# Attention times input weights as seven block products for batches 2 to 4, their right operands split once and kept in scratch memory

## The chip, the cores and the metric

The kernel runs on one core of a Trainium2 chip. The metric is the device time of one execution in microseconds (us), lower is better. The engines named below are PE (TensorE: matmuls; PEld are its weight loads), DVE (VectorE), ACT (ScalarE), POOL (GpSimd) and SP (SyncE); POOL and SP only issue DMAs in the part that is changed.

## The reference

Four batches (b = 0 to 3) of q, k and v with N = 6080 rows and C = 256 columns; the attention is over channels, so its matrix is 256 x 256. The result of the attention goes through a feed-forward layer with squared ReLU.

```python
qn = q / (norm(q, axis=1) + 1e-6)          # per batch and column
kn = k / (norm(k, axis=1) + 1e-6)
a  = softmax(kn.T @ qn / tau)              # 256 x 256 per batch; the sum has + 1e-9
x  = v @ a                                 # 6080 x 256
h  = x @ w_in                              # w_in 256 x 2048
out = (maximum(h, 0) ** 2) @ w_out         # w_out 2048 x 256
```

## The kernel before

The kernel doesn't compute x. For each batch it folds the attention into the weights, W = a @ w_in (256 x 2048), and takes h = v @ W. Every matmul operand that must be exact is split into a high and a low fp32r part, and a product is three matmuls, high by high, high by low and low by high.

The rows of a batch are cut into six chunks, five of T = 512 and one of T = 480 column pairs (1024 or 960 rows, 24 chunks in all), and the 2048 columns of W into eight blocks j. A chunk with a block is a **quad**, the unit in which all is placed: 192 quads, numbered 0 to 191, 48 to a batch. Layer 1 of a quad is a Strassen-Winograd product of 2 x 2 blocks: seven block products m1 to m7 of three matmuls each (`product`, L395), whose results pass PSUM banks named h, x and z and are summed by ACT copies (x L429, z L438, m L450) and DVE adds (s L455). ACT and DVE square the ReLU and split it into g high and g low (r L404/L405, g L406/L407 and, for the second half, L416 on DVE, g high L417 on ACT, g low L418 on DVE). Layer 2 (`layer2`, L490) takes 24 matmuls of a quad's g with wo's high and low half (woh, wol), one quad later, on the output banks o. That is 45 matmuls to a quad.

The block sums that layer 1 needs of W are made by `combine` for a **group** g of two blocks: DVE adds, then for each of the two blocks a weight tile wt that ACT casts (L323, high halves) and DVE subtracts (L324, low halves), stored by POOL to the scratch wsc (L326). Each quad loads its weight tile from there on SP's queue (`load_wt`, L332), issued 1.5 quads ahead. wt is a ring of three buffers that these tiles under construction share with the loaded ones.

While a batch runs, the next batch b is prepared beside it. `at(u, f, ...)` hands f to the scheduler at u, in quads; with end = 30 + 48 (b - 1), the scores (L180, 12 matmuls of 256 columns a quad) run up to quad `end`, then norms, exps and `attnT` (transposes, quad end + 2.46). Then comes the fold of the four groups: their inputs are loaded (`load_win`, SP), split into high and low (`fold_split`, ring hl, L286/L287) and multiplied in two halves of six matmuls each (`fold`, L302), one half in each of two quads; the result is scaled by the softmax's denominator as ACT copies it from PSUM (L305, buffer kqt). MID is 0.46.

The order of the instructions on each engine is fixed at build time by the scheduler from these places. The rings that matter are wt (3 buffers), kqt (3), hl (3), sq (2), and two PSUM banks h. SP and POOL issue their DMAs in program order, and a DMA that has to wait holds up those behind it.

Of the kernel before, what the change touches and what calls it, by code (L numbers as in the profile page):

```python
# [8 lines left out]
F32 = mybir.dt.float32  # L9
F32R = mybir.dt.float32r  # L10
# [6 lines left out]
P = 128  # L17
# [3 lines left out]
def tile_channel_attention_relu2_ffn(ctx, tc, kq, vT, tau, w_in, w_out, outT):  # L21
# [85 lines left out]
    win = {}  # L107
# [33 lines left out]
    kqt = {}  # L141
# [41 lines left out]
    def score_add(b, s):  # L183
        if b in s_acc:
            nc.vector.tensor_add(out=s_acc[b], in0=s_acc[b], in1=s)
        else:
            s_acc[b] = small.tile([P, NH * C], F32, name="s_acc")
            nc.vector.tensor_copy(out=s_acc[b], in_=s)

    def score_burst(b, kts):  # L190
# [13 lines left out]
    def norms(b):  # L204
        a = accs[b][:, 0]
        nc.vector.tensor_add(out=a, in0=a, in1=accs[b][:, 1])
        nps = h_bank()
        for i in range(2 * NH):
            nc.tensor.matmul(out=nps[:, i:i + 1], lhsT=a[:, i * P:(i + 1) * P], rhs=ones[:, 0:1],
                             start=True, stop=True)  # L210
        n2 = nps[:, :2 * NH]
        y = small.tile([P, 2 * NH], F32, name="y")
        z = small.tile([P, 2 * NH], F32, name="z")
        nc.scalar.activation(out=y, in_=n2, func=AF.Sqrt)
        nc.scalar.activation(out=root, in_=y[:, 0:1], func=AF.Exp, scale=0.0)
        x = y
        y = small.tile([P, 2 * NH], F32, name="y2")
        nc.vector.tensor_scalar_max(out=y, in0=x, scalar1=1e-30)
        nc.vector.reciprocal(out=z, in_=y)
        nc.vector.tensor_mul(out=z, in0=z, in1=n2)  # L220
        nc.vector.tensor_add(out=y, in0=y, in1=z)
        nc.vector.tensor_scalar(out=y, in0=y, scalar1=0.5, scalar2=1e-6, op0=ALU.mult, op1=ALU.add)
        nc.vector.reciprocal(out=z, in_=y)
        nc.vector.tensor_scalar_mul(out=z[:, :NH], in0=z[:, :NH], scalar1=rtau)
        diag = small.tile([P, NH, P], F32, name="diag")
        for d in range(NH):
            nc.vector.tensor_scalar_mul(out=diag[:, d], in0=ident, scalar1=z[:, NH + d:NH + d + 1])
        attn[b, "z"] = z, diag
# [10 lines left out]
    def exps(b, s):  # L239
        z, zq = attn[b, "z"]  # L240
        den = small.tile([P, NH], F32, name="den", bufs=2)
        attn[b, "e"] = []
        for h in range(NH):
            e = small.tile([P, C], F32, name="e", bufs=2)
            nc.vector.scalar_tensor_tensor(out=e, in0=s[:, h * C:(h + 1) * C], scalar=z[:, h:h + 1],
                                           op0=ALU.mult, in1=zq, op1=ALU.mult)
            nm = small.tile([P, 1], F32, name="nm", bufs=2)
            nc.vector.tensor_reduce(out=nm, in_=e, op=ALU.max, axis=AX.X, negate=True)
            nc.scalar.activation(out=e, in_=e, func=AF.Exp, bias=nm, scale=1.0, accum_out=den[:, h:h + 1])
            attn[b, "e"].append(e)  # L250
        nc.vector.tensor_scalar_add(out=den, in0=den, scalar1=1e-9)
        nc.vector.reciprocal(out=den, in_=den)
        attn[b, "den"] = den

    def attnT(b):
        aT = h_bank()
        aTv = aT.rearrange("p (d c) -> p d c", d=NH)
        for h, e in enumerate(attn[b, "e"]):
            for d in range(NH):
                nc.tensor.transpose(out=aTv[:, d, h * P:(h + 1) * P], in_=e[:, d * P:(d + 1) * P],  # L260
                                    identity=ident)
        aTh = small.tile([P, NH, C], F32R, name="aTh")
        aTl = small.tile([P, NH, C], F32R, name="aTl")
        nc.scalar.copy(out=aTh, in_=aTv)
        nc.vector.tensor_sub(out=aTl, in0=aTv, in1=aTh)
        attn[b] = aTh, aTl


    NP = 7
    A11, A12, A22, S2, S3, S1, S4 = range(NP)  # L270
    wt = {}
    wi = {}
    us = {}
    wsc = {}

    def load_win(b, g):
        win[b, g] = work.tile([P, NH, 2, GW], F32, name="kqt", tag="kqt", bufs=KB)
        nc.sync.dma_start(out=win[b, g], in_=wins[g])

    def fold_split(b, g):  # L280
        W = win.pop((b, g))
        wi[b, g] = []
        for d in range(NH):
            w = work.tile([P, 2, 2 * GW], F32R, name="hl", tag="hl", bufs=HB)
            x = W[:, d].rearrange("p t f -> p (t f)")
            (nc.vector.tensor_copy if b else nc.scalar.copy)(out=w[:, 0], in_=x)  # L286
            nc.vector.tensor_sub(out=w[:, 1], in0=x, in1=w[:, 0])  # L287
            wi[b, g].append(w)

    def fold(b, g, ch, ps=None):  # L290
        aTh, aTl = attn[b]
        if ch == 0:
            tag, n = ("kqt", KB) if b or g else ("vt", VB)
            us[b, g] = work.tile([P, NH, 2, GW], F32, name=tag, tag=tag, bufs=n)
        u = us[b, g]
        cs = slice(ch * P, (ch + 1) * P)
        if ps is None:
            ps = h_bank()
        n = 0
        for d in range(NH):  # L300
            for l, r in ((aTh, 0), (aTh, 1), (aTl, 0)):
                nc.tensor.matmul(out=ps, lhsT=l[:, d, cs], rhs=wi[b, g][d][:, r, :],  # L302
                                 start=n == 0, stop=n == 3 * NH - 1)
                n += 1
        nc.scalar.activation(out=u[:, ch].rearrange("p t f -> p (t f)"), in_=ps, func=AF.Copy,  # L305
                             scale=attn[b, "den"][:, ch:ch + 1])

    def combine(b, g):

# [8 lines left out]
        for i in range(2):  # L318
            j = 2 * g + i
            w = work.tile([P, 2, NP, P], F32R, name="wt", bufs=WB)  # L320
            js = slice(i * P, (i + 1) * P)
            for o, x in ((w[:, :, 0:2], u[:, :, 0, js]), (w[:, :, 2:3], u[:, 1:2, 1, js]), (w[:, :, 3:7], S[:, :, js])):
                nc.scalar.copy(out=o[:, 0], in_=x)  # L323
                eng.tensor_sub(out=o[:, 1], in0=x, in1=o[:, 0])  # L324
            wsc[b, j] = scratch.tile([P, 2, NP, P], F32, name=f"wsc{j}", bufs=2)
            nc.gpsimd.dma_start(out=wsc[b, j], in_=w.bitcast(F32))  # L326
# [13 lines left out]
    vt = {}  # L340
# [190 lines left out]
    s1 = ps_o.tile([P, HMAX], F32, name="o11")  # L531
# [48 lines left out]
    for b in range(1, B):  # L580
        u0 = (b - 1) * QB
        first, last = (NJ + 2 if b == 1 else 0), 30
        for i in range(NT // 2):
            u, k = u0 + first + i * (last - first) // (NT // 2), 2 * i
            if k % G == 0:
                at(u - 3.4, score_load, b, k // G)
            at(u - 0.8, score_norm, b, k)
            if b > 1 or k >= EARLY * G:
                at(u - 1.0, score_split, b, k)
                at(u - 0.5, score_split, b, k + 1)  # L590
                at(u + MID, score_burst, b, [k, k + 1])
        end = u0 + last
        at(end + MID, norms, b)
        at(end + 1 + MID, spread, b)
        at(end + 1.6, lambda b=b: exps(b, s_acc[b]))
        at(end + 2 + MID, attnT, b)
        for g in range(NG):
            u = end + 3 + 4 * g
            at(u - 3.0, load_win, b, g)
            at(u - 0.5, fold_split, b, g)  # L600
            at(u + MID, fold, b, g, 0)
            at(u + 1 + MID, fold, b, g, 1)
            at(u + 1.7, combine, b, g)
    for n, (ci, j) in enumerate(quads):
        if ci:
            at(n - 1.5, load_wt, ci, j)
# [61 lines left out]
```

## Time and profile before

| | |
|---|---|
| median of 3 runs | 2172.79 us (2172.06 to 2174.04) |
| the profiled execution | 2172.03 us, its span 2170.2 us |
| granted TensorE clock | 1.00 |
| PE busy | 2156.8 us, 99% of the span |
| DVE, ACT, POOL busy | 1568.7, 1389.2 and 70.1 us |
| DMA | 323.08 MB, mean 149 GB/s |

The profiled execution is 0.76 us below the median, and its span starts and ends inside it: 1.8 us lie around the span. Matmuls overlap, so the length of one (0.39 us) is not what it costs; that is read from start to start.

### The profile page before, as it was taken

Reading aid. Unit: us, or ns where it says so; the run is one execution under the profiler, and the core shown is the slowest. Engines: PE = TensorE matmul, PEld = TensorE weight load, DVE = VectorE, ACT = ScalarE, POOL = GpSimd, SP = SyncE. Lnnn points to the kernel's source line nnn. Section 1 sums busy time; section 2 is a strip of 40 time slices with the busy share of each in tenths; the row PEclk is TensorE's granted clock in tenths of the full one; section 3 lists DMA queues with packets and bytes.
Section 4 is the critical chain, followed back from the end, with each engine's and each line's share of the span. In section 5 each row is a group of like instructions: output and inputs, shape, how many; then the busy total and the mean of one; then the engine's idle time right before and its main releaser. Section 6 shows DMA issues by size and latency. Waiting matters only on the chain.

```text
span 2170.2 us, 26050 instructions
## 1 busy us (share of the span) xinstructions
PE 2156.8 (99%) x9908; PEld 1806.2 (83%) x9908; DVE 1568.7 (72%) x2252; ACT 1389.2 (64%) x2359; POOL 70.1 (3%) x135
## 2 busy tenths in 40 slices
PE   9999999999999999999999999999999999999999
PEld 8778888888888888888888888888888888888887
DVE  6897788776787777876678778777677666666665
ACT  5786767666666666665676766666566565566564
POOL 0000000000000000000000000000000000000000
PEclk9999999999999999999999999999999999999999
DMA  9755534245364343334535434333344342343331
GB/s 341 269 199 182 192 114 153 84 167 193 125 217 151 134 162 106 115 113 148 187 144 209 163 124 148 112 124 133 129 154 156 133 141 105 104 140 104 104 122 53
DMA packets 61917, 323.08 MB, mean 149 GB/s; under 512 B 7328, under 2 KB 9888, under 8 KB 55008
## 3 DMA queue, kind: packets, MB, share of 16 engines
q1 hardware_dynamic: 49440, 266.03, 35.4%
q0 software_dynamic: 12352, 55.39, 6.5%
q8 instruction: 78, 1.28, 0.2%
q14 instruction: 47, 0.39, 0.1%
HBM read 265.03 MB, written 56.36 MB: 148 GB/s over the span
## 4 chain that ended last, share of the span: by engine, by line
PE 62%; issue 32%; DVE 2%; DMA 1%; POOL 1%; ACT 1%; SPq 0%; POOLq 0%; DVEq 0%; ACTq 0%
PE o L490 30%; PE h L395 15%; PE z L395 8%; PE x L395 4%; PE h L180 2%; PE x L180 2%; PE h L302 1%; POOL outT L496 1%; DMA kqt<-kq 1%; POOL wsc L326 0%; DMA wsc<-wt 0%; DVE vt L373 0%; DVE s L455 0%; DVE wt L324 0%; DVE hl L101 0%
## 5 line engine op out<-in xcount | busy, mean ns | idle before, releaser
L490 PE MATMUL o<-g,woh 128*128 128x512 f32 (+1 forms) x3072 | 1065.4, 388 | 1.9 <-DVE g L418 1.0
L490 PEld LDWEIGHTS o<-g,woh 128*128 128x128 f32 x3072 | 576.0, 188 | 120.6 <-DVE g L418 2.2
L395 PE MATMUL h<-vt,wt 128*128 128x512 f32 (+1 forms) x2304 | 614.9, 388 | 1.5 <-ACT x L429 1.5
L490 PE MATMUL o<-g,wol 128*128 128x512 f32 (+1 forms) x1536 | 594.8, 387 | 0.0
L395 PEld LDWEIGHTS h<-vt,wt 128*128 128x128 f32 x2304 | 431.7, 188 | 91.1 <-ACT x L429 3.4
L417 ACT CAST g<-s 128x1024 fp32r<-128x1024 f32 (+1 forms) x192 | 199.1, 1037 | 320.4 <-DVE s L416 320.1
L407 DVE TENSOR_TENSOR g<-r,g 128x512 fp32r<-128x512 f32 (+1 forms) x384 | 263.1, 685 | 155.6 <-ACT g L406 150.9
L490 PEld LDWEIGHTS o<-g,wol 128*128 128x128 f32 x1536 | 288.3, 188 | 57.2
L395 PE MATMUL z<-vt,wt 128*128 128x512 f32 (+1 forms) x1152 | 324.8, 389 | 0.4 <-ACT z L438 0.4
L418 DVE TENSOR_TENSOR g<-s,g 128x1024 fp32r<-128x1024 f32 (+1 forms) x192 | 233.0, 1213 | 123.1 <-ACT g L417 122.5
L405 ACT ACTIVATE r<-r 128x512 f32<-128x512 f32 (+1 forms) x384 | 241.2, 628 | 6.9
L395 PEld LDWEIGHTS z<-vt,wt 128*128 128x128 f32 x1152 | 212.1, 188 | 39.3 <-ACT z L438 0.8
L404 ACT ACTIVATE r<-z 128x512 f32<-128x512 f32 (+1 forms) x192 | 113.3, 590 | 202.3 <-PE z L395 201.0
L416 DVE SCALAR_TENSOR_TENSOR s<-s 128x1024 f32<-128x1024 f32 (+1 forms) x192 | 232.3, 1210 | 1.1
L406 DVE CAST g<-r 128x512 fp32r<-128x512 f32 (+1 forms) x192 | 81.8, 426 | 188.3 <-ACT r L405 187.4
L395 PE MATMUL x<-vt,wt 128*128 128x512 f32 (+1 forms) x576 | 160.8, 387 | 0.0
L455 DVE TENSOR_TENSOR s<-z,m 128x512 f32<-128x512 f32 (+1 forms) x192 | 130.5, 680 | 19.7 <-PE z L395 19.6
L438 ACT COPY z<-h 128x512 f32<-128x512 f32 (+1 forms) x192 | 110.3, 574 | 50.7 <-PE h L395 50.3
L161 DVE TENSOR_TENSOR acc<-acc,sq 128x1024 f32<-128x1024 f32 x92 | 112.7, 1225 | 28.8 <-ACT sq L160 26.5
L455 DVE TENSOR_TENSOR s<-h,m 128x512 f32<-128x512 f32 (+1 forms) x192 | 130.2, 678 | 0.0
L395 PEld LDWEIGHTS x<-vt,wt 128*128 128x128 f32 x576 | 108.1, 188 | 21.6
L404 ACT ACTIVATE r<-x 128x512 f32<-128x512 f32 (+1 forms) x192 | 113.6, 592 | 10.2
(112 smaller groups left out, 1757.3 us busy)
## 6 DMA issues: line engine op xcount, KB each, us to landing
wt<-wsc SPq DMA_DIRECT2D x184, 896.0 KB, 4.6
kqt<-kq SPq DMA_DIRECT2D x47, 1024.0 KB, 6.6
wsc<-wt POOLq DMA_DIRECT2D x32, 896.0 KB, 5.5
v<-vT SPq DMA_DIRECT2D x40, 512.0 KB, 5.6
outT<-res POOLq DMA_DIRECT2D x80, 256.0 KB, 5.0
g<-kq SPq DMA_DIRECT2D x6, 1024.0 KB, 10.5
kqt<-wins SPq DMA_DIRECT2D x12, 512.0 KB, 6.6
v<-vT SPq DMA_DIRECT2D x8, 480.0 KB, 4.4
```

What stands on the lines that cost most here:

```text
L161: nc.vector.tensor_add(out=accs[b], in0=accs[b], in1=sq)
L180: nc.tensor.matmul(out=s[:, h * C:(h + 1) * C], lhsT=l, rhs=r, start=first and h == 0 and n == 0, stop=last and n == len(terms) - 1, skip_ ...
L395: nc.tensor.matmul(out=out[:, :T], lhsT=w[:, l, i], rhs=v[:, r, :T], start=start and n == 0, stop=n == 2, skip_group_check=True)
L404: nc.scalar.activation(out=r[:, :T], in_=ps[:, :T], func=AF.Relu)
L405: nc.scalar.activation(out=r[:, :T], in_=r[:, :T], func=AF.Square)
L407: nc.vector.tensor_sub(out=hl[:, 1, :T], in0=r[:, :T], in1=hl[:, 0, :T])
L416: nc.vector.scalar_tensor_tensor(out=s, in0=s, scalar=0.0, op0=ALU.max, in1=s, op1=ALU.mult)
L417: nc.scalar.copy(out=h, in_=s)
L418: nc.vector.tensor_sub(out=l, in0=s, in1=h)
L438: nc.scalar.copy(out=st["Z"][:, :T], in_=st["B"][:, :T])
L455: ins = nc.vector.tensor_add(out=state[q]["s"][:, i, :T], in0=ps[:, :T], in1=state[q]["m7"][:, :T])
L490: nc.tensor.matmul(out=o[:, :T], lhsT=l[:, wg, wj, es], rhs=r[:, :T], start=first and k == 0, stop=last and k == 2)
```

## The change

Batch 0 is folded as before. For b = 1 to 3 the groups are taken in two **pairs** (g = 0 and 2, with u = end + 3 and end + 10), and each pair's 256 x 512 by blocks is one Strassen-Winograd product of 2 x 2 blocks: seven products of three matmuls, 512 columns wide (`fold7`, L362), one product in each of 14 quads in a row. The left operands, seven 128 x 128 blocks or block sums of the attention's transpose, are made and split in `attnT`. The right operands are blocks and block sums of w_in; `right7` makes and splits them for b = 1 and stores the split tiles to a scratch tsc on POOL's queue, and for b = 2 and 3 loads them from there on SP's queue, 2.5 quads ahead. DVE adds and ACT copies collect the seven results. The softmax's denominator is applied to e on DVE, ahead of the transposes. `combine` is unchanged, but both groups of a pair are now combined one after the other at the pair's end (quads end + 10 and end + 10.6; end + 17 and end + 17.6), where before each group was combined in its own second quad (end + 4.7, and every fourth quad on). The tiles diag and e move into another ring.

```diff
     def attnT(b):
...
+        a11, a12, a21, a22 = a[:, 0, :P], a[:, 1, :P], a[:, 0, P:], a[:, 1, P:]
+        nc.vector.tensor_add(out=s1, in0=a21, in1=a22)
+        nc.vector.tensor_sub(out=s2, in0=s1, in1=a11)
+        nc.vector.tensor_sub(out=s3, in0=a11, in1=a21)
+        nc.vector.tensor_sub(out=s4, in0=a12, in1=s2)
+        for o, x in ((w[:, :, 0:2], a[:, :, :P]), (w[:, :, 2:3], a[:, 1:2, P:]), (w[:, :, 3:7], S)):
+            nc.scalar.copy(out=o[:, 0], in_=x)
+            nc.vector.tensor_sub(out=o[:, 1], in0=x, in1=o[:, 0])
+        attn[b] = w
...
+    ORDER = (A11, A12, S4, S2, S1, S3, A22)
...
+    def right7(b, g, k):
+        hl = right[b, g, k] = work.tile([P, 2, 2 * GW], F32R, name="hl", tag="hl", bufs=HB)
+        if b > 1:
+            nc.sync.dma_start(out=hl.bitcast(F32), in_=tsc[g, k])
+            return
...
+        nc.scalar.copy(out=hl[:, 0], in_=x)
+        nc.vector.tensor_sub(out=hl[:, 1], in0=x, in1=hl[:, 0])
+        if B > 2:
+            tsc[g, k] = scratch.tile([P, 2, 2 * GW], F32, name=f"tsc{g}_{k}")
+            nc.gpsimd.dma_start(out=tsc[g, k], in_=hl.bitcast(F32))
+
+    def fold7(b, g, k):
+        i = ORDER[k]
+        r = right.pop((b, g, k))
+        ps = h_bank()
+        for n, (l, m) in enumerate(((0, 0), (0, 1), (1, 0))):
+            nc.tensor.matmul(out=ps, lhsT=attn[b][:, l, i], rhs=r[:, m], start=n == 0, stop=n == 2)
...
+        if i == A11:
+            nc.scalar.copy(out=U, in_=ps)
+        elif i == A12:
+            add(out=c11, in0=U, in1=ps)
+        elif i == S4:
+            nc.scalar.copy(out=c12, in_=ps)
+        elif i == S2:
+            add(out=U, in0=U, in1=ps)
+        elif i == S1:
+            add(out=V, in0=U, in1=ps)
+            add(out=c12, in0=c12, in1=V)
+        elif i == S3:
+            add(out=c22, in0=V, in1=ps)
+            add(out=U, in0=U, in1=ps)
+        else:
+            add(out=c21, in0=U, in1=ps)
...
-        for g in range(NG):
-            u = end + 3 + 4 * g
-            at(u - 3.0, load_win, b, g)
-            at(u - 0.5, fold_split, b, g)
-            at(u + MID, fold, b, g, 0)
-            at(u + 1 + MID, fold, b, g, 1)
-            at(u + 1.7, combine, b, g)
+        for g in range(0, NG, 2):
+            u = end + 3 + 3.5 * g
+            if b == 1:
+                at(u - 3.5, load_wins2, g)
+            for i in range(NP):
+                at(u + i - (0.7 if b == 1 else 2.5), right7, b, g, i)
+                at(u + i + MID, fold7, b, g, i)
+            at(u + NP, combine, b, g)
+            at(u + NP + 0.6, combine, b, g + 1)
```

Three places show how instructions move. Names carry the number of a tile; the lines of the changed kernel are L362 (fold7), L404 (casts of combine), L407 (stores), L413 (weight loads), L476 (layer 1), L571 (layer 2).

On PE, the middle of a quad with a fold before (the second half of a group of batch 1):

```order
L490 MATMUL o_3752<-g_4154,wol 128x512
L490 MATMUL o_3752<-g_4154,woh 128x512
L302 MATMUL h<-hl,aTh 128x512 x2
L302 MATMUL h<-hl,aTl 128x512
L302 MATMUL h<-hl,aTh 128x512 x2
L302 MATMUL h<-hl,aTl 128x512
L395 MATMUL z<-vt,wt 128x512 x3
L395 MATMUL h<-vt,wt 128x512 x3
```

and the same quad after:

```order
L571 MATMUL o_3763<-g_4167,wol 128x512
L571 MATMUL o_3763<-g_4167,woh 128x512
L362 MATMUL h<-hl,aT 128x512 x3
L476 MATMUL z<-vt,wt 128x512 x3
L476 MATMUL h<-vt,wt 128x512 x3
```

Six matmuls have become three, at the same place of the quad.

On PE, quad 49 before, from the product x to the score matmuls (L180) of batch 2; each o takes the matmuls with g's high part (woh), wol, and last the low part of g with woh:

```order
L395 MATMUL x<-vt,wt 128x512 x3
L490 MATMUL o_5251<-g_5205,woh 128x512
L490 MATMUL o_5251<-g_5205,wol 128x512
L490 MATMUL o_5251<-g_5205,woh 128x512
L490 MATMUL o_5255<-g_5205,woh 128x512
L490 MATMUL o_5255<-g_5205,wol 128x512
L490 MATMUL o_5255<-g_5205,woh 128x512
L180 MATMUL h<-hl 128x256 x12
L395 MATMUL z<-vt,wt 128x512 x3
```

and after:

```order
L476 MATMUL x<-vt,wt 128x512 x3
L180 MATMUL h<-hl 128x256 x4
L571 MATMUL o_5324<-g_5278,woh 128x512
L571 MATMUL o_5324<-g_5278,wol 128x512
L571 MATMUL o_5328<-g_5278,woh 128x512
L571 MATMUL o_5328<-g_5278,wol 128x512
L180 MATMUL h<-hl 128x256 x8
L476 MATMUL z<-vt,wt 128x512 x2
L571 MATMUL o_5324<-g_5278,woh 128x512
L571 MATMUL o_5328<-g_5278,woh 128x512
L476 MATMUL z<-vt,wt 128x512
```

The two matmuls with the low part of g have moved behind all score matmuls and two of z.

On ACT, the casts of a weight tile that waits for the store of the one before, and what stands behind them, before (the group at quads 34 and 35):

```order
L323 CAST wt_3906<-kqt_3776 128x256 [waits DMASW4_49,DVE_49]
L323 CAST wt_3906<-kqt_3776 128x128
L323 CAST wt_3906<-sq_3892 128x512
L404 ACTIVATE r_3995<-z_3951 128x512 [waits DVE_49,PE_49]
L417 CAST g2_3979<-s_3971 128x1024 [waits DVE_49]
L429 COPY x_4008<-h_4004 128x512 [waits PE_49]
```

and after (the second group of the first pair, quads 41 and 42):

```order
L404 CAST wt_4481<-kqt_3796 128x256 [waits DMASW3_49,DVE_49]
L404 CAST wt_4481<-kqt_3796 128x128
L404 CAST wt_4481<-sq_4476 128x512 [waits DVE_49]
L485 ACTIVATE r_4605<-z_4549 128x480 [waits DVE_49,PE_49]
L404 CAST wt_4490<-kqt_3796 128x256 [waits DMAHW3_49,DMAHW0_49]
L404 CAST wt_4490<-kqt_3796 128x128
L404 CAST wt_4490<-sq_4476 128x512
L510 COPY x_4618<-h_4614 128x480 [waits PE_49]
```

The cast that waits for a store (a DMASW semaphore) is now followed by another tile's casts ahead of the copy x. On SP, the weight loads of quads 41 to 44 are after:

```order
L413 DMA wt_4348<-wsc1_430 128x1792 [waits DMAHW0_49,PE_49]
L427 DMA v_4414<-vT 128x1024 [waits DVE_49]
L427 DMA v_4414<-vT 128x1024 [waits DMAHW5_49]
L413 DMA wt_4466<-wsc2_632 128x1792 [waits DMAHW1_49,DMASW6_49,DMAHW6_49,DVE_49,PE_49]
L148 DMA kqt_4853<-kq 128x2048 [waits DVE_49]
L413 DMA wt_4581<-wsc3_641 128x1792 [waits DMASW5_49,DMAHW2_49,DMASW3_49,PE_49]
L413 DMA wt_4669<-wsc4_855 128x1792 [waits DMASW6_49,DMAHW3_49,DVE_49,PE_49]
```

and before:

```order
L332 DMA wt_4346<-wsc1_431 128x1792 [waits DMAHW7_49,PE_49]
L346 DMA v_4389<-vT 128x1024 [waits DMAHW3_49,DVE_49,Activation_49]
L346 DMA v_4389<-vT 128x1024
L332 DMA wt_4435<-wsc2_633 128x1792 [waits DMASW7_49,DMAHW6_49,DMASW6_49,Activation_49]
L332 DMA wt_4526<-wsc3_642 128x1792 [waits DMAHW1_49,PE_49]
L278 DMA kqt_4565<-wins3_93 128x1024 [waits DMASW1_49]
L148 DMA kqt_4803<-kq 128x2048 [waits DMAHW0_49,DVE_49]
L332 DMA wt_4612<-wsc4_856 128x1792 [waits DMAHW2_49,PE_49]
```

The loads that wait for weight stores (DMASW) stand at quads 42, 43 and 44 after, and at quad 42 before, one of four such places of batch 1.

More of the change, by code (lines that the diff above doesn't have):

```diff
@@ L194, in score_burst @@
         score_add(b, s)
+    NP = 7
+    A11, A12, A22, S2, S3, S1, S4 = range(NP)
     attn = {}
@@ L224, in norms @@
         nc.vector.tensor_scalar_mul(out=z[:, :NH], in0=z[:, :NH], scalar1=rtau)
-        diag = small.tile([P, NH, P], F32, name="diag")
+        diag = work.tile([P, HMAX], F32, name="tt", tag="tt", bufs=TB)[:, :C].rearrange("p (d c) -> p d c", d=NH)
         for d in range(NH):
@@ L243, in exps @@
         for h in range(NH):
-            e = small.tile([P, C], F32, name="e", bufs=2)
+            e = work.tile([P, HMAX], F32, name="tt", tag="tt", bufs=TB)[:, :C]
             nc.vector.scalar_tensor_tensor(out=e, in0=s[:, h * C:(h + 1) * C], scalar=z[:, h:h + 1],
@@ L253, in exps @@
         attn[b, "den"] = den
+        if b:
+            for h, e in enumerate(attn[b, "e"]):
+                nc.vector.tensor_scalar_mul(out=e, in0=e, scalar1=den[:, h:h + 1])
     def attnT(b):
@@ L261, in attnT @@
                                     identity=ident)
[L262 to L270, printed above, removed]
+        w = small.tile([P, 2, NP, P], F32R, name="aT")
+        if b == 0:
+            aTh, aTl = attn[b] = [w[:, i, :2 * NH].rearrange("p (d h) c -> p d (h c)", d=NH) for i in range(2)]
+            nc.scalar.copy(out=aTh, in_=aTv)
+            nc.vector.tensor_sub(out=aTl, in0=aTv, in1=aTh)
+            return
+        a = work.tile([P, NH, C], F32, name="sq", tag="sq")
+        S = work.tile([P, 4, P], F32, name="sq", tag="sq")
+        s2, s3, s1, s4 = (S[:, i] for i in range(4))
+        nc.scalar.copy(out=a, in_=aTv)
+        a11, a12, a21, a22 = a[:, 0, :P], a[:, 1, :P], a[:, 0, P:], a[:, 1, P:]
[7 more added lines that the diff above has]
+        attn[b] = w
     wt = {}
@@ L274, in tile_channel_attention_relu2_ffn @@
     wsc = {}
-    def load_win(b, g):
-        win[b, g] = work.tile([P, NH, 2, GW], F32, name="kqt", tag="kqt", bufs=KB)
-        nc.sync.dma_start(out=win[b, g], in_=wins[g])
     def fold_split(b, g):
@@ L285, in fold_split @@
             x = W[:, d].rearrange("p t f -> p (t f)")
-            (nc.vector.tensor_copy if b else nc.scalar.copy)(out=w[:, 0], in_=x)
+            nc.scalar.copy(out=w[:, 0], in_=x)
             nc.vector.tensor_sub(out=w[:, 1], in0=x, in1=w[:, 0])
@@ L292, in fold @@
         if ch == 0:
-            tag, n = ("kqt", KB) if b or g else ("vt", VB)
+            tag, n = ("kqt", KB) if g else ("vt", VB)
             us[b, g] = work.tile([P, NH, 2, GW], F32, name=tag, tag=tag, bufs=n)
@@ L306, in fold, with load_wins2 @@
                              scale=attn[b, "den"][:, ch:ch + 1])
+    assert NG % 2 == 0
+    ORDER = (A11, A12, S4, S2, S1, S3, A22)
+    wins2 = {}
+    right = {}
+    tsc = {}
+    sums = {}
+    def load_wins2(g):
+        t = wins2[g] = work.tile([P, 2, NH, 2 * GW], F32, name="kqt", tag="kqt", bufs=KB)
+        for i in range(2):
+            nc.sync.dma_start(out=t[:, i], in_=wins[g + i].rearrange("p h t f -> p h (t f)"))
+    def right7(b, g, k):
+        hl = right[b, g, k] = work.tile([P, 2, 2 * GW], F32R, name="hl", tag="hl", bufs=HB)
+        if b > 1:
+            nc.sync.dma_start(out=hl.bitcast(F32), in_=tsc[g, k])
+            return
+        t = wins2[g]
+        b11, b12, b21, b22 = t[:, 0, 0], t[:, 1, 0], t[:, 0, 1], t[:, 1, 1]
+        if ORDER[k] == S2:
+            nc.vector.tensor_sub(out=b12, in0=b12, in1=b11)
+            nc.vector.tensor_sub(out=b22, in0=b22, in1=b12)
+        if ORDER[k] == S3:
+            nc.vector.tensor_sub(out=b11, in0=b22, in1=b11)
+        if ORDER[k] == A22:
+            nc.vector.tensor_sub(out=b21, in0=b21, in1=b22)
+        x = {A11: b11, A12: b21, S4: b22, S2: b22, S1: b12, S3: b11, A22: b21}[ORDER[k]]
+        nc.scalar.copy(out=hl[:, 0], in_=x)
[3 more added lines that the diff above has]
+            nc.gpsimd.dma_start(out=tsc[g, k], in_=hl.bitcast(F32))
@@ new lines, in fold7 @@
+    def fold7(b, g, k):
[5 more added lines that the diff above has]
+        if i == A11:
+            sums[b, g] = (work.tile([P, 2, NH, 2 * GW], F32, name="kqt", tag="kqt", bufs=KB),
+                          work.tile([P, 2, 2 * GW], F32, name="sq", tag="sq"))
+        u, uv = sums[b, g]
+        c11, c21, c12, c22 = u[:, 0, 0], u[:, 0, 1], u[:, 1, 0], u[:, 1, 1]
+        U, V = uv[:, 0], uv[:, 1]
+        add = nc.vector.tensor_add
+        if i == A11:
+            nc.scalar.copy(out=U, in_=ps)
[13 more added lines that the diff above has]
+            add(out=c21, in0=U, in1=ps)
+            for j in range(2):
+                us[b, g + j] = u[:, j].rearrange("p h (t f) -> p h t f", t=2)
```

## Prediction

> **What bounds the kernel now.** I read the head of the page first, then the chain that ended last.
>
> ```profile
> PE 2156.8 (99%) x9908; PEld 1806.2 (83%) x9908; DVE 1568.7 (72%) x2252; ACT 1389.2 (64%) x2359; POOL 70.1 (3%) x135
> PEclk9999999999999999999999999999999999999999
> PE 62%; issue 32%; DVE 2%; DMA 1%; POOL 1%; ACT 1%; SPq 0%; POOLq 0%; DVEq 0%; ACTq 0%
> ```
>
> TensorE is busy for 99% of the span at an unreduced clock. The chain is PE and its own issue for 94%; everything else together holds 6% of it. Up to quad 30, three before the one that starts at 441.53 us below, the order of every engine is the same before and after. So two things can move the time: the number of matmuls, and the short waits of PE after 400 us. The timeline of PE over two quads with a fold (quads 33 and 34), and of a quad start in the narrower chunk, gives the price of a matmul. Columns: start, length, then the operation.
>
> ```profile
> 441.53 1.52 PE L395 MATMUL h<-vt,wt 128*128 128x512 f32 x6
> 446.97 0.62 PE L302 MATMUL h<-hl,aTh 128*128 128x512 f32 x2
> 447.42 0.39 PE L302 MATMUL h<-hl,aTl 128*128 128x512 f32 x1
> 447.65 0.62 PE L302 MATMUL h<-hl,aTh 128*128 128x512 f32 x2
> 448.10 0.39 PE L302 MATMUL h<-hl,aTl 128*128 128x512 f32 x1
> 448.33 0.84 PE L395 MATMUL z<-vt,wt 128*128 128x512 f32 x3
> 453.09 1.52 PE L395 MATMUL h<-vt,wt 128*128 128x512 f32 x6
> ...
> 550.67 1.46 PE L395 MATMUL h<-vt,wt 128*128 128x480 f32 x6
> ...
> 560.42 1.46 PE L395 MATMUL h<-vt,wt 128*128 128x480 f32 x6
> ```
>
> Six fold matmuls start at 446.97 and the product goes on at 448.33: 1.36 us, or 0.227 us each, with nothing between. A quad with a fold lasts 11.56 us (441.53 to 453.09), so one without it 10.20; in the 480-wide chunk a bare quad lasts 9.75 (550.67 to 560.42). The waits of PE's weight loads from 400 us on (in total, times, longest):
>
> ```profile
> PEld o L490 <- DVE g L418: 2.2, 3, 1.4
> PEld h L395 <- ACT x L429: 1.3, 2, 1.0
> PEld o L490 <- ACT g L417: 1.2, 2, 0.7
> PEld o L490 <- DVE g L407: 0.3, 1, 0.3
> ```
>
> They sum to 5.0 us: all that better placement of side work can win. Two places make up most of it, quad 49 (first fence) and quad 136 (second); a bracket is the idle time before and its releaser.
>
> ```profile
> 618.22 0.39 PE L490 MATMUL o<-g,wol 128*128 128x512 f32 x1
> 619.58 0.73 PE L490 MATMUL o<-g,woh 128*128 128x512 f32 x2 [0.97 <-DVE g L418]
> ...
> 618.31 1.22 DVE L418 TENSOR_TENSOR g<-s,g 128x1024 fp32r<-128x1024 f32 x1
> ```
>
> ```profile
> 1588.64 0.61 ACT L323 CAST wt<-kqt 128x256 fp32r<-128x256 f32 x2 [2.41 <-DMA wsc<-wt]
> ...
> 1591.17 0.39 PE L490 MATMUL o<-g,woh 128*128 128x512 f32 x1
> 1592.09 0.91 PE L395 MATMUL h<-vt,wt 128*128 128x480 f32 x3 [0.53 <-ACT x L429]
> ```
>
> In quad 49 PE reaches the low half of g before DVE has subtracted it: 1.36 us between starts where 0.23 is usual, 1.1 lost. In quad 136 ACT sat 2.41 us in its queue on a cast into a weight tile whose buffer was still being stored, its copies for the product came late, and PE lost 0.7 here and 0.8 in small gaps behind it, 1.5 in all.
>
> **The change part by part.** *Matmuls.* A batch folded on the fly (1, 2, 3) has 48 fold matmuls before (4 groups of 2 times 6) and 42 after (2 pairs of 7 times 3). 18 fewer, by 0.227 us: **-4.1 us**. They lie on PE's saturated path with nothing beside them. The Trainium skill ("TensorE: Matmul & The Clock Gate", Back-to-back issue gap) gives 131 ns per matmul for a sustained stream with weight loads at 512 columns; by it the term would be an estimated -2.4 us. The rows above contradict it at 227 ns, and the rows decide.
>
> *DVE and ACT.* The groups of the operations removed, and of those that price the new ones:
>
> ```profile
> L302 PE MATMUL h<-hl,aTh 128*128 128x512 f32 x124 | 39.8, 395 | 1.5 <-DVE hl L287 0.9 <-ACT hl L286 0.6
> L305 ACT ACTIVATE kqt<-h,den 128x512 f32<-128x512 f32 x30 | 20.6, 690 | 36.0 <-PE h L302 35.8
> L166 ACT CAST hl<-kqt 128x512 fp32r<-128x512 f32 x120 | 74.3, 621 | 33.2 <-PE h L180 28.8 <-PE h L302 0.9
> L286 DVE CAST hl<-kqt 128x512 fp32r<-128x512 f32 x24 | 9.4, 424 | 0.0
> L287 DVE TENSOR_TENSOR hl<-kqt,hl 128x512 fp32r<-128x512 f32 x24 | 16.2, 688 | 0.0
> ```
>
> The first row also shows that PE hardly waited for a split fold operand (1.5 us in 124, from the first batch, whose fold stays). ACT loses 24 scaled copies (24 x 0.690 = -16.6 us) and gains 14 casts (x 0.621 = +8.7), 15 plain copies (at most 0.690, +10) and a few small ones: about +3 us. DVE loses 24 casts (-10) and 10 subtractions (-7), and gains 50 adds or subtractions 512 wide (50 x 0.688 = +34), 12 of 128 columns and 6 scalings (about 7 more): about +25 us. Both engines have 600 to 780 us idle in the span, so the sum costs nothing; only the place can. A product's PSUM bank is drained by one or two DVE adds or an ACT copy, and with two banks in turn its next user is the h of the next quad, 453.09 - 446.97 = 6.1 us after: two adds (1.4 us) behind two DVE operations of 1.22 us fit. Cost 0; without that cover at most 0.7 us for each of 42 drains.
>
> *attnT.* Four small sums and a three-part split stand between the transposes (quad 32.46) and the first product (33.46), about one quad, 10 us, for about 4 us of work: 0, at most 1.5.
>
> *Scratch transfers.* The right operands go out 14 times (512 KB, POOL) and come in 28 times (SP), for 8 input loads of 512 KB less. The load of this size and the two weight transfers:
>
> ```profile
> kqt<-wins SPq DMA_DIRECT2D x12, 512.0 KB, 6.6
> wt<-wsc SPq DMA_DIRECT2D x184, 896.0 KB, 4.6
> wsc<-wt POOLq DMA_DIRECT2D x32, 896.0 KB, 5.5
> 441.53:537.00 95.47, 95.47 (x425) 79.38 (x424) 66.05 (x104) 59.88 (x107) 5.10 (x10) 1.00 0.47 170
> ```
>
> The last row is the stage of quads 33 to 41 (us; busy PE, PEld, DVE, ACT, POOL; clock, DMA share, GB/s): the DMA engines are under half busy and DVE 69%. A right operand is asked for 2.5 quads ahead, 25 us against 6.6. On SP's queue it waits for the product three before it and holds back a weight load by up to half a quad (5 us); that load goes out 1.5 quads (15 us) ahead and needs 4.6. Cost 0, with 5 us to spare; if the queue slipped by more, the excess would fall on PE once a quad. POOL is 3% busy; its 14 more issues matter only to the stores behind them.
>
> *Combines and the weight ring.* This is the unknown term. Before, each of four groups writes its two weight tiles through one ring buffer, three quads before a load needs it. After, two groups are combined back to back at the end of a pair (quads 40 and 47), and at four places (quads 41 to 43, 48 to 50, 96 to 98, 144 to 146) a buffer must be filled, stored, filled, stored and loaded within two quads. The first group before, at quads 34 and 35, shows the legs; then come issue to landing of all weight stores (min, median, max) and of all weight loads, and the starts of quads 48 and 49:
>
> ```profile
> 465.38 0.40 ACT L323 CAST wt<-kqt 128x256 fp32r<-128x256 f32 x1
> 468.53 0.54 POOL L326 DMA_DIRECT2D wsc<-wt  x1 [25.27 <-DVE wt L324]
> 472.44 0.61 ACT L323 CAST wt<-kqt 128x256 fp32r<-128x256 f32 x2 [1.72 <-DVE g L407]
> 475.88 0.54 POOL L326 DMA_DIRECT2D wsc<-wt  x1 [6.81 <-DVE wt L324]
> ...
> DMA to landing us min/median/max: 3.8/5.5/12.3
> ...
> DMA to landing us min/median/max: 4.3/4.6/11.3
> ...
> 602.20 1.54 PE L395 MATMUL h<-vt,wt 128*128 128x512 f32 x6
> ...
> 613.86 1.56 PE L395 MATMUL h<-vt,wt 128*128 128x512 f32 x6
> ```
>
> First cast to first store 3.2 us, to the second cast 3.9, to the second store 3.4, store 5.5, load 4.6: 20.6 us. At 41 to 43 there are two 480-wide quads with three fold matmuls each, 2 x (9.75 + 0.68) = 20.9; at 48 to 50 and 96 to 98 two with score matmuls, 2 x 11.66 (602.20 to 613.86) = 23.3; at 144 to 146 two bare ones, 20.4. ACT takes its queue in order: behind the second tile's waiting cast stand the next r, then the copies x and m of a product that PE waits for, so a late store blocks PE twice, as in quad 136; and POOL's weight stores stand behind scratch and output stores. With the casts queued behind ACT's product copies I take a stall of +0.8 at quad 43 and +0.5 over the other three. Bounds: 0 (legs at 3.8 us) and 21.7 (second store at 12.3, then 27.4 us of chain against 20.9, 23.3, 23.3 and 20.4). Nearest is the median leg.
>
> *Old stalls.* In the new order the low-half matmuls of quad 49 stand behind the score matmuls and the first of z, 2.5 us later than in the row at 618.22: -1.1. The group whose cast blocked ACT into quad 136 is gone, and the new combine there has three tiles for its buffer and no load that is due in two quads: -1.5. The rest of the 5.0 us stays in kind, and I add +0.6 for waits that the order doesn't show, as the DMA wait of quad 136 was not to be seen in it. Stalls: 0.8 + 0.5 - 1.1 - 1.5 + 0.6 = **-0.7**.
>
> **Sum.** The profiled execution took 2172.03 us (span 2170.2): 2172.03 - 4.1 - 0.7 = 2167.2. It lies 0.76 under the median of the runs, 2172.79, so the forecast is **2168.0 us**. About 0.2% (4.3 us) is what a measurement tells from no change: faster is below 2168.4, slower above 2177.1.
>
> **The rivals.**
> *Stalls gone altogether:* combines lie at two places of a batch, not four, and if the ring holds, all 5.0 us may go and none come: 2172.8 - 4.1 - 4.0 to 5.0 = 2164 to 2165. For it: each stall shown has its cause removed. Against: two combines in a row put 9 us of DVE work where layer 2 is due.
> *Gain eaten at the boundaries:* store legs of 8 us instead of 5.5 make the chains 23.1: 2.2 at quad 43, 2.7 at 146; DVE late for g in quads 48, 96 or 144 adds what quad 49 lost before, 1.1. Against a base of 2166.7 (the forecast without its 1.3 of chains) that is 2172 or so. For it: DVE g L418 is the largest wait already.
> *Slower, the ring:* the same mechanism with the second store at 9.5 us or more at all four places (3.7 + 1.3 + 1.3 + 4.2 = 10.5) ends above 2177.1; at the longest leg of the trace 2166.7 + 21.7 = 2188. For it: the scratch stores share POOL's queue with the weight stores, and legs up to 12.3 exist. Against: the median leg and a DMA share of 0.47. The Trainium skill ("DMA: Bandwidth & Descriptors", Issuing engines are not separate DMA queues) says that transfers started by different engines run on the same 16 DMA engines and interleave; by it the new stores and loads lengthen these legs wherever they overlap. No run here shows it yet.
> *The matmuls save less:* at the skill's 131 ns the sum ends at 2169.7. By the rows above, 227 ns at every place looked at, this is all but excluded.
>
> **How the numbers follow.** Forecast 0.42 (its own range 2166.5 to 2170), stalls gone 0.22, gain eaten 0.24, slower 0.10, smaller saving 0.02. Faster by over 0.2%: 0.22 and 0.25 of the forecast's 0.42, 0.47. Slower: 0.10. Within: 0.43. The range 2164 to 2174 takes in the first three and leaves out the ring and some edges of the others.
>
> **What would show it.** 18 fewer layer-1 and fold matmuls at 0.227; fold quads 10.9 us instead of 11.56 or 10.20; no PE wait on DVE g at quad 49 and none on ACT x at 136; a wait of at most 2.5 us at quad 43; ACT's wait for weight stores near its present size. The prediction is wrong if weight loads end late at 43 or 146, or if quads 48 and 96 stall on g by more than 1 us each.

## The result: 1% slower, and the profile after

The changed kernel takes 2194.54 us (median of 5 runs, 2191.67 to 2197.51) against 2172.79 us before (5 runs, 2171.27 to 2174.04): 1.0100 times the time, 95% interval 1.0088 to 1.0111. The forecast was 2168.0, with 2164 to 2174 as its range and 0.10 for slower. Its profiled execution took 2193.19 us, with a span of 2191.4. The head of its page and the chain that ended last:

```profile
PE 2158.7 (99%) x9890; PEld 1804.4 (82%) x9890; DVE 1589.8 (73%) x2292; ACT 1386.9 (63%) x2370; POOL 77.5 (4%) x149
PE 49%; issue 45%; DMA 2%; POOL 2%; DVE 2%; ACT 0%; SPq 0%; POOLq 0%; DVEq 0%; ACTq 0%
```

PE has 18 instructions less (9890 against 9908) and yet is busy 1.9 us longer; DVE's busy time grew by 21 us and ACT's fell by 2, where +25 and +3 were worked out. The busy line says nothing of the 21 us. The waits of PE's weight loads from 400 us on do:

```profile
PEld h L476 <- issue: 10.7, 3, 5.7
PEld z L476 <- DVE s L536: 5.7, 2, 3.2
PEld h L476 <- PE h L476: 2.7, 2, 1.4
PEld o L571 <- DVE g L499: 2.2, 4, 1.2
PEld o L571 <- DVE g L488: 1.8, 1, 1.8
PEld h L476 <- PE o L571: 1.1, 1, 1.1
PEld h L476 <- DMA wt<-wsc: 1.0, 1, 1.0
```

Where 5.0 us stood before, these seven rows are 25.2 (26.8 with three small ones). A wait put down to "issue" hides a late weight load here, as the timeline of quad 43 shows. The rows are, in order of time, ACT's cast of the second tile that goes through the free buffer, the weight loads on SP's queue, and PE:

```profile
532.14 0.40 ACT L404 CAST wt<-kqt 128x256 fp32r<-128x256 f32 x1
...
540.70 0.61 ACT L404 CAST wt<-kqt 128x256 fp32r<-128x256 f32 x2 [3.50 <-DMA wsc<-wt]
...
550.99 0.33 SPq L413 DMA_DIRECT2D wt<-wsc  x1
...
552.39 0.37 PE L571 MATMUL o<-g,woh 128*128 128x480 f32 x1
558.06 2.74 PE L476 MATMUL h<-vt,wt 128*128 128x480 f32 x6 [5.30 <-DMA wt<-wsc]
```

It is the chain that the prediction priced at 20.6 us: fill, store, fill, store, load. From the first cast (532.14) to PE's start (558.06) it took 25.9. Its fills cost what was said (3.1 and 3.0 us); its transfers did not: first store 5.4 us instead of 3.9, second 7.1 instead of 5.5, load 6.9 instead of 4.6, by issue and landing in the trace. And the six matmuls behind the wait took 2.74 us where 1.46 is usual.

Quad 48 shows the second form, of stores that hold up engines in front of PE. POOL issues the second store, ACT waits for it, DVE for ACT, PE for DVE:

```profile
613.28 0.53 POOL L407 DMA_DIRECT2D wsc<-wt  x1 [5.82 <-DVE wt L405]
...
622.07 0.60 ACT L404 CAST wt<-kqt 128x256 fp32r<-128x256 f32 x2 [4.01 <-DMA wsc<-wt]
...
622.51 0.42 DVE L405 TENSOR_TENSOR wt<-kqt,wt 128x256 fp32r<-128x256 f32 x1 [3.81 <-ACT wt L404]
...
623.59 0.96 PE L476 MATMUL z<-vt,wt 128*128 128x512 f32 x3 [2.08 <-DVE s L536]
```

The window from that store's issue to its landing, 8.8 us (busy time of PE, PEld, DVE, ACT, POOL; granted clock, DMA share, GB/s):

```profile
613.30:622.05 8.75, 8.21 (x43) 6.64 (x41) 5.23 (x8) 4.76 (x8) 1.06 (x2) 1.00 0.94 317
```

The DMA engines are 94% busy, so something runs beside the store. DVE's subtraction for the weight tile stands in its queue ahead of the s that frees PE's bank z, and so PE waits for a weight tile that it will not use for several quads.

By the length of the quads in the two traces (fold quads against what they take without waits), the difference of 21.2 us in span comes out so:

| where | us |
|---|---|
| ahead of quad 0, a first load of k and q that landed late in this execution (the other profiles: 0.0 to 1.0, and 3.0 in the first of the two kernels with four buffers) | +2.9 |
| 18 fold matmuls | -4.1 |
| quads 42 and 43; 90 and 91 | +7.2; +4.4 |
| quads 48 and 49; 96 and 97 | +4.1; +4.9 |
| quad 145 | +3.7 |
| quads 136 and 144 (the stalls of before there are gone) | -2.1 |
| quad 32 (attnT), quad 0, small ones | +0.5 |
| behind the last quad | -0.3 |

### The profile page after: what moved, and what is told of

It reads as the page before. It is cut to its first block, busy times and chain, and to the rows that moved or that the text cites. A ratio compares the mean times of both kernels' runs of the same rounds, so it can differ in the third digit from the quotient of the medians.

```text
span 2191.4 us, 26162 instructions
## 1 busy us (share of the span) xinstructions
PE 2158.7 (99%) x9890; PEld 1804.4 (82%) x9890; DVE 1589.8 (73%) x2292; ACT 1386.9 (63%) x2370; POOL 77.5 (4%) x149
## 4 chain that ended last, share of the span: by engine, by line
PE 49%; issue 45%; DMA 2%; POOL 2%; DVE 2%; ACT 0%; SPq 0%; POOLq 0%; DVEq 0%; ACTq 0%
PE o L571 24%; PE h L476 12%; PE z L476 6%; PE x L476 3%; PE x L180 2%; PE h L180 2%; POOL outT L577 1%; DMA wt<-wsc 1%; DMA kqt<-kq 1%; POOL wsc L407 0%; DMA wsc<-wt 0%; PE h L316 0%; DVE hl L101 0%; DMA kqt<-w_out 0%; PE o L180 0%
## 5 line engine op out<-in xcount | busy, mean ns | idle before, releaser
L571 PE MATMUL o<-g,woh 128*128 128x512 f32 (+1 forms) x3072 | 1066.0, 388 | 2.7 <-DVE g L488 1.9
L571 PEld LDWEIGHTS o<-g,woh 128*128 128x128 f32 x3072 | 576.2, 188 | 121.4 <-DVE g L488 2.9
L476 PE MATMUL h<-vt,wt 128*128 128x512 f32 (+1 forms) x2304 | 617.9, 390 | 13.8 <-DMA wt<-wsc 10.9
L571 PE MATMUL o<-g,wol 128*128 128x512 f32 (+1 forms) x1536 | 595.0, 387 | 0.0
L476 PEld LDWEIGHTS h<-vt,wt 128*128 128x128 f32 x2304 | 432.7, 188 | 105.9 <-issue 10.7
L571 PEld LDWEIGHTS o<-g,wol 128*128 128x128 f32 x1536 | 288.5, 188 | 57.4
L476 PE MATMUL z<-vt,wt 128*128 128x512 f32 (+1 forms) x1152 | 325.0, 389 | 5.3 <-DVE s L536 4.9
L499 DVE TENSOR_TENSOR g<-s,g 128x1024 fp32r<-128x1024 f32 (+1 forms) x192 | 232.8, 1212 | 130.0 <-ACT g L498 129.4
L476 PEld LDWEIGHTS z<-vt,wt 128*128 128x128 f32 x1152 | 211.8, 188 | 45.1 <-DVE s L536 5.7
L476 PE MATMUL x<-vt,wt 128*128 128x512 f32 (+1 forms) x576 | 160.8, 387 | 0.0
L476 PEld LDWEIGHTS x<-vt,wt 128*128 128x128 f32 x576 | 108.1, 188 | 21.5
```

What stands on the lines that cost most here:

```text
L476: nc.tensor.matmul(out=out[:, :T], lhsT=w[:, l, i], rhs=v[:, r, :T], start=start and n == 0, stop=n == 2, skip_group_check=True)
L499: nc.vector.tensor_sub(out=l, in0=s, in1=h)
L571: nc.tensor.matmul(out=o[:, :T], lhsT=l[:, wg, wj, es], rhs=r[:, :T], start=first and k == 0, stop=last and k == 2)
```

## The experiments

The theories. **Ring:** combining two groups back to back sends four weight tiles through the one free weight buffer, and its chain is late. **Scratch:** the stores and loads of the right operands lengthen the weight transfers. **Load:** the new DVE and ACT work is too much where it stands. The ratio given is that to the kernel before on the same chip.

**1. Combines spread.**

```diff
-            at(u + NP + 0.6, combine, b, g + 1)
+            at(u + NP + 3, combine, b, g + 1)
```

> The changed kernel, with the second combine of each pair moved from 0.6 to 3 quads after the first (quads 43 and 50 instead of 40.6 and 47.6); nothing else. Ring theory (two combines back to back push four weight tiles through the one free weight buffer within two quads): the waits at quads 43, 91, 48 to 50, 96 to 98 and 145 (about 24 us with the slow restart) shrink to a few us, time 2168 to 2175. Scratch theory (the right operands' stores and loads lengthen the weight stores): the waits stay, 2188 or more. Load theory (the new DVE work is too much at the boundary): the same DVE work is there, only spread, so part of the gain, 2178 to 2188.

Measured: 2165.18 us, ratio 0.9969 (0.9957 to 0.9981). All its waits of PE's weight loads from 400 us on:

```profile
PEld o L571 <- DVE g L499: 1.0, 4, 0.4
PEld h L476 <- ACT x L510: 1.0, 1, 1.0
PEld o L571 <- ACT g L498: 0.3, 1, 0.3
PEld h L266 <- DVE tt L259: 0.3, 1, 0.3
```

and its busy line:

```profile
PE 2150.2 (99%) x9890; PEld 1801.9 (83%) x9890; DVE 1590.7 (74%) x2292; ACT 1387.0 (64%) x2370; POOL 77.6 (4%) x149
```

2.6 us of waits are left of 26.8, with the same work on every engine and the same scratch transfers. Load and scratch can't explain the loss; the place of the second combine can. The kernel is faster than before, and a little faster than the ring theory had it.

The distance does not shorten the stores. The second store of a combine still takes 8.3 us at quads 48 and 96 (8.8 and 9.5 in the changed kernel), and up to 10.1 us elsewhere. ACT also waits for weight stores almost as long as in the changed kernel, where it is 22.3 us; first the kernel before, then the spread one:

```profile
ACT wt L323 <- DMA wsc<-wt: 10.8, 6, 2.4
ACT wt L404 <- DMA wsc<-wt: 18.5, 6, 5.0
```

What differs is the store that is waited for. In the changed kernel each of the six waits is for the second store of the group combined first (5.4 to 9.5 us); in the spread kernel, as in the kernel before, each is for the first store of a group (3.8 to 5.8 us), and only one of the six holds PE in the spread kernel, by 0.7 us in quad 147. No cast waits for a long store any more.

**2. The reverse on the kernel before:** only its combines are moved, to the changed kernel's places.

```diff
-            at(u + 1.7, combine, b, g)
+            at(end + (10, 10.6, 17, 17.6)[g], combine, b, g)
```

> The kernel before, with its four groups' combines moved to the places of the changed kernel (end + 10, 10.6, 17 and 17.6 instead of end + 4.7, 8.7, 12.7 and 16.7); the fold stays at 48 matmuls and there is no scratch for right operands. Ring theory: the waits of the changed kernel appear here too, 15 to 25 us: 2184 to 2198. Scratch theory and load theory (neither the transfers nor the new DVE work are here): 2172 to 2177.

Measured: 2201.58 us, ratio 1.0131 (1.0115 to 1.0147), above the range given. Quad 48 of it, ACT, DVE and PE:

```profile
621.26 0.60 ACT L323 CAST wt<-kqt 128x256 fp32r<-128x256 f32 x2 [5.87 <-DMA wsc<-wt]
...
621.70 0.43 DVE L324 TENSOR_TENSOR wt<-kqt,wt 128x256 fp32r<-128x256 f32 x1 [5.91 <-ACT wt L323]
...
622.78 0.96 PE L395 MATMUL z<-vt,wt 128*128 128x512 f32 x3 [3.92 <-DVE s L455]
```

The same wait, with no block product and no scratch for right operands in the kernel. The place alone costs 29 us here, all of it in the quads around the moved combines (42 and 43, 48 to 50, 90 and 91, 96 and 97, 138 and 145).

**3. No scratch.** Every batch splits its own right operands; the stores to and the loads from tsc are left out.

> The changed kernel without the scratch for right operands: every batch loads the input weights and splits its own seven right operands, so no scratch store or load is left (14 stores and 28 loads of 512 KB less, 16 input loads more, and casts and subtractions for two more batches). Scratch theory: the waits at quads 43 and 91 vanish and those at the boundaries shrink, 2168 to 2176. Ring theory: only the legs that overlapped a scratch transfer get shorter, by 1 to 3 us at quads 43 and 91, the boundaries stay: 2186 to 2196. Load theory: more DVE work, slower than 2194.5.

Measured: 2194.23 us, ratio 1.0102 (1.0086 to 1.0118). The scratch theory is out as the main cause: without those 42 transfers the wait at quad 43, where nothing takes the place of the stores, falls only from 5.4 to 4.7 us; that at 91, in a batch that has its own input loads and splits instead, rises from 2.9 to 4.9.

**4. Four weight buffers**, in two ways to find the room.

```diff
-    WB = 3
+    WB = 4
```

> The changed kernel with four weight buffers instead of three; the room comes from one v-combination buffer (9 to 8), one output buffer (3 to 2) and one buffer of m7 (2 to 1). Ring theory: the waits for weight tiles go, 2168 to 2172 plus what the three lost buffers cost (unknown, by the rows of before where each is rarely waited for, 0 to 5): 2168 to 2177. Scratch theory and load theory: the waits stay, 2190 to 2197.

> The changed kernel with four weight buffers, the room now from one v-combination buffer (9 to 8) and one buffer of g's first half (3 to 2), the output and m7 buffers as they were. Ring theory: the waits of the output copies in the other four-buffer kernel (6.3 us and their slow restarts) came from its output buffers, so they go, and the weight waits stay small: 2168 to 2175. If it stays at 2184, the back-to-back combines cost something that a fourth buffer doesn't lift (transfers that meet, or the smaller buffers).

Measured: 2183.89 us (1.0051, 1.0033 to 1.0069) and 2185.53 us (1.0064, 1.0047 to 1.0081). Neither came to what the ring theory gave (2168 to 2177 and 2168 to 2175); the second is the case that the last sentence of its expectation names. The ring's own waits did go, but for 2.5 us that PE still waits for a weight load at quad 43 in the first of the two. ACT's wait for weight stores was this in the changed kernel,

```profile
ACT wt L404 <- DMA wsc<-wt: 22.3, 6, 4.8
```

and is this in the second of the two:

```profile
ACT wt L404 <- DMA wsc<-wt: 0.8, 2, 0.5
```

But DVE and PE at its quad 49 show a new wait:

```profile
623.51 0.66 DVE L575 COPY res<-o 128x480 f32<-128x480 f32 x1 [6.33 <-DMA outT<-res]
...
625.36 1.22 PE L571 MATMUL o<-g,woh 128*128 128x512 f32 x2 [5.37 <-DVE g L499]
```

With a buffer more, the four stores go out closer together (13.7 us from the first to the last, 21.8 in the changed kernel) and meet the loads of weights, v, k and q. The output stores behind them land after 11.7 us, DVE waits for an output buffer, and the low half of g, behind it in DVE's queue, holds PE. The first of the two kernels, with an output buffer less, waits there as well, on ACT (res L575, 6.3 us). So the back-to-back combines have two costs: the ring's chain, and a burst of transfers that remains when the ring is widened.

**5. Spread and four buffers together.**

> Four weight buffers (room as in the second four-buffer kernel) and the combines 3 quads apart. If the 6 us waits at quads 49 and 97 with four buffers came from four stores meeting the other transfers at once, they go here: 2163 to 2168. If they came from the smaller buffers of v combinations and g: they stay, 2178 to 2185.

Measured: 2172.05 us, ratio 0.9998 (0.9989 to 1.0007), between the two expectations. The 6 us waits are gone with the same smaller buffers, so they came from the burst. The fourth buffer and the room taken for it together cost the 7 us to the spread kernel (PE waits 9.2 us for DVE's g L499, in 17 pieces of at most 1.8); which of the smaller buffers it is was not separated.

**6. Only the first pair spread.**

> The changed kernel with the second combine put off to 3 quads only in the first pair of each batch (quad 43); the second pair is still combined back to back (47 and 47.6). If the places are independent: the waits at quads 43 and 91 with their slow restarts go (5.4 + 1.7 + 2.9 + 1.5 = 11.5 us), those at 48 to 50, 96 to 98 and 145 stay: 2181 to 2185. If one pile-up feeds the next, less than 2180.

Measured: 2180.42 us, ratio 1.0038 (1.0023 to 1.0053): 14.1 us less than the changed kernel, where quads 42, 43, 90 and 91 held 11.6. That is 0.6 us under the range. In the two traces those four quads are together 11.6 us shorter and no other quad differs by more than 0.6, so the pairs are nearly independent; the rest of the 14.1 lies outside them (1.9 us ahead of quad 0 in these two executions).

**7. What lengthens the transfers?** First v's loads were to be moved from quad 48.

> The changed kernel with each chunk's load of v (two transfers of 512 KB) asked for 2 quads later, so that it no longer starts beside the second weight store after quad 48; the combines stay back to back. If the stores are long because v runs beside them: the second store at quad 48 falls from 8.8 to 4 to 6 us and the waits at 48, 96 (2.2 and 2.9 us, with 1 us behind each) go, the rest stays: 2184 to 2190. If v doesn't matter: 2191 to 2197.

Measured: 2194.46 us, ratio 1.0102 (1.0087 to 1.0117). It tells nothing: in its trace v's two transfers still start between the first and second store after quad 48, as before the edit (SP's queue has them at the same place). So v was left out from the fourth chunk on:

```diff
+        if ci > 2:
+            raw_v[ci] = kept[0]
+            return
```

> The changed kernel, combines back to back, that loads v for the first three chunks only and uses the third chunk's v for all later ones: the 42 later v transfers of 512 KB are left out, everything computed from them stays in place. If the second store at quads 48 and 96 is long because v's load runs beside it: it falls from 8.8 and 9.5 us to 4 to 6, and the wait of ACT for it (4 us), of DVE and of PE behind it (2.5 and 3.2 us, and 1.3 after each) go: 2182 to 2188; quads 43, 50, 91 and 145 stay. If the leg's length has another cause: 2192 to 2196.

Measured: 2184.74 us, ratio 1.0056 (1.0042 to 1.0070), in the range given if v is the cause. Issue to landing of the second store at quads 48 and 96 falls from 8.8 and 9.5 us to 4.4 in both. ACT's wait for weight stores:

```profile
ACT wt L404 <- DMA wsc<-wt: 9.7, 3, 3.6
```

and PE at quad 48, where the product z now starts without a wait:

```profile
620.27 0.37 PE L576 MATMUL o<-g,woh 128*128 128x480 f32 x1
620.48 0.86 PE L481 MATMUL z<-vt,wt 128*128 128x512 f32 x3
```

So v's loads lengthen the store at quads 48 and 96. The total is not v's alone: in the two traces quads 48, 49, 96 and 97 are 7.9 us shorter and quad 145 by 1.9, the start ahead of quad 0 by 2.9, but quads 42, 43, 90 and 91 are 5.2 us longer. The waits at 43 and 50, where v does not run, stay (5.7 and 1.6 us); that at 91 grows from 2.9 to 5.2, which was not followed. For quads 43 and 91 the largest other loads in the window are those of the next batch's k and q; they were halved.

> The changed kernel, combines back to back, whose k and q loads for batches 3 and 4 bring half of the bytes (512 KB instead of 1 MB each, the scores of these batches use the loaded half twice); everything else stays. If these loads lengthen the legs at quads 43 and 91: the second store and the weight load there fall from 7.1 and 6.9 us by 1 to 2 us each, and PE's waits of 5.4 and 2.7 us by 2 to 4 us, with the slow restart partly gone; some also at quads 50 and 98: 2183 to 2190. If the legs are long from the weight stores and loads among themselves: the waits at 43 and 91 stay, 2191 to 2196.

Measured: 2188.98 us, ratio 1.0076 (1.0058 to 1.0094), within the first expectation, but with little of its mechanism: at quad 43 the second store falls from 7.1 to 5.7 us, yet the weight load rises from 6.9 to 8.0, and PE's wait there falls only from 5.4 to 5.0. At quad 91 it falls from 2.9 to 2.0. The two profiled executions are 3.0 us apart, and 2.2 of that lie ahead of quad 0; quads 90 and 91 gain 2.3 us, and quad 138 loses 1.2 to a new wait for a weight load, though batch 4 has no next batch to load. So the loads of k and q are a share of the wait at quad 91 and hardly one of that at quad 43. The other transfers in these windows are the weight stores and loads themselves and those of the right operands (0.8 us at quad 43 by experiment 3); what lengthens the legs there was not separated further.

**8. How far apart?** With the second group first, 2 quads apart; and with the first group first, 2 and 4.

> The changed kernel with the pair's second group combined first, 0.8 quads before the pair's end (it is complete one product earlier), and the first group 1.2 quads after the end: 2 quads between the combines instead of 0.6, 3 in the kernel that spread them. Ring theory: two tiles (fill 3, store 4 to 5 each) take some 16 us of the free buffer, and with 2 quads (21 us) between combines little is left late: 2166 to 2175. If 3 quads are needed: 2178 to 2190.

> The changed kernel with the combines 2 quads apart (first group first) instead of 0.6. Ring theory: two tiles take 16 to 20 us of the free buffer and 2 quads are 20.4 to 23.3 us: mostly relieved, 2165 to 2175.

> The changed kernel with the combines 4 quads apart instead of 0.6, as far apart as in the kernel before. Ring theory: at 3 quads only 0.8 us of waits over 0.5 us are left after 400 us, so no more to win: 2164 to 2167. A gain here would say that 3 quads still leave a wait that the profile doesn't show; a loss, that the sums' buffer, held longer, delays the next batch's loads.

Measured, beside 0.6 quads (2194.54) and 3 (2165.18):

| apart | us | ratio |
|---|---|---|
| 2, second group first | 2179.33 | 1.0035 (1.0022 to 1.0048) |
| 2 | 2168.51 | 0.9979 (0.9970 to 0.9988) |
| 4 | 2167.07 | 0.9974 (0.9964 to 0.9983) |

2 quads take away nearly all of it; the intervals of 2, 3 and 4 overlap, so these can't be told apart surely. The other order misses its range. At quad 90 ACT waited 11.35 us for the first store of the group combined last, which landed 8.9 us after its issue, and PE waited for the copy x behind it:

```profile
1081.22 0.60 ACT L404 CAST wt<-kqt 128x256 fp32r<-128x256 f32 x2 [11.35 <-DMA wsc<-wt]
...
1084.21 1.57 PE L476 MATMUL h<-vt,wt 128*128 128x480 f32 x3 [4.89 <-ACT x L510]
```

Why that order fares worse at the same distance was not followed.

## Why the prediction was wrong

**The matmuls: right.** Fold quads of the changed kernel last 10.88 us, as said, and three fold matmuls take their 0.68 us:

```profile
450.04 0.84 PE L362 MATMUL h<-hl,aT 128*128 128x512 f32 x3
450.72 0.84 PE L476 MATMUL z<-vt,wt 128*128 128x512 f32 x3
```

The term of -4.1 us is in the account above, and 227 ns held against the 131 that the prediction gives from the Trainium skill ("TensorE: Matmul & The Clock Gate", Back-to-back issue gap).

**Old stalls: right.** In the spread kernel, where nothing covers them, quad 49 is 1.2 us shorter than before and quad 136, apart from the product now in it, by 1.6. Matmuls and stalls together give -7.5 us there by the medians.

**DVE, ACT, attnT, scratch: right** in that they cost nothing that can be told: the spread kernel carries all of them and gains. With the combines back to back, the scratch stores take 0.8 us at quad 43. attnT took 0.4 us of PE in quad 32, within 0 to 1.5.

**The step that failed is the weight ring**, the term "+0.8 at quad 43 and +0.5 over the other three". The mechanism and the four places were named, and as the rival "Slower, the ring" it ended at 2188 with the longest leg of the trace; at these four it measured 20 us against 1.3 (7.2, 4.1, 4.9 and 3.7, the old stall of quad 49 already taken off). Three parts of it:

- *The legs.* The chain's first store was priced at 3.9 us, by the row at 468.53, which is the first store of a group; at the new places a second store stands there, that of the group combined first. The two kinds differ. In the kernel before, after 400 us, first stores took 3.8 to 5.8 us and second ones 5.3 to 12.3, 6.8 at the median, and the two longest, 12.3 and 11.3, were issued at quads 48 and 96, two of the four new places. In the changed kernel this store took 5.4 us at quad 41 and 8.8, 9.5 and 9.0 at quads 48, 96 and 144. The store behind it, priced at the median of 5.5, took 7.1, 3.9, 3.9 and 3.9, and the load, priced at 4.6, took 6.9, 10.4, 9.6 and 6.8. Against such legs stood the 47% that the DMA engines are busy on the average of that stage; in the window of quad 48 it was 94%. So long second stores are old; new is that a cast waits for them.
- *The queues.* That a late store blocks PE twice was written down, but priced at nothing in the sum. At quads 48 and 96 it is the larger part: the load that ends the chain came 1.7 and 0.9 us late, but ahead of that the second store had stopped ACT for 4 us, DVE behind ACT and PE behind DVE.
- *The place thought safe.* Quads 90 and 91 were left out of the four, and no reason was given. They cost 4.4 us. Quads 136 to 139, where the prediction saw no load due within two quads, cost nothing.

The rival's sentence that the scratch transfers would lengthen the legs was wrong in its object: the rule it cites (the Trainium skill, "DMA: Bandwidth & Descriptors", Issuing engines are not separate DMA queues) agrees with the traces, in that POOL's store took 8.8 us beside SP's loads of v and 4.4 without them, but the transfers that mattered most were old ones, met at a new place.

## What to carry to other kernels

When a change moves a step that fills, stores and reloads shared buffers, price its transfers with what else is in flight at the new place, not with the median of the old places, and price a late transfer also at every queue in which an instruction waits for it. Where a change wins on one term and loses on its side steps, moving the side steps alone, in both kernels, separates them: here one number (0.6 to 3 quads between two combines) turned +1.0% into -0.3%. More buffers are not the same cure as more distance, since the transfers then come closer together.

## What the runs showed of the hardware

A long wait of PE costs more than its length. After PE's longest wait in the changed kernel the matmuls started 400 ns apart instead of 217, and the granted clock of that window was 0.57 (the number ahead of the DMA share):

```profile
557.50:561.50 4.00, 3.44 (x9) 2.95 (x10) 0.00 (x0) 1.73 (x4) 0.00 (x0) 0.57 0.86 360
```

Over all the profiles of this study, after 400 us, the 14 gaps of 3.2 us or more between two starts of PE were all followed, at once or within 2 us, by 7 or more matmuls at about half speed, the 26 gaps of 1.2 to 2.2 us by none, and of the 20 between them 9 were followed by some. One such restart cost 1.5 us in the changed kernel (eight starts from 558.06 on, 3.3 us instead of 1.7). The Trainium skill ("TensorE: Matmul & The Clock Gate", What's actually happening) says that the clock is at half speed after at least one idle window of about 3.4 us, and that the window runs freely. The 12 gaps of 3.8 us and more agree; that shorter ones, from 2.2 us on, did it in 11 cases is outside its words, and there the measurement decides.
